# Attention of layer B with the keys on partitions in packed tiles, softmax sums from a ones matrix, and a layernorm by Ln and Exp

## The chip, the cores and the metric

The kernel runs on one core of one Trainium2 chip. The metric is the device time of one execution in microseconds (us). A kernel is run several times and its median is quoted. Engines are called as the profile calls them: PE is TensorE's matmul stream, PEld its weight loads, DVE is VectorE, ACT is ScalarE, POOL is GpSimd.

## The reference, cut to what matters

The network is four layers, A, B, A, B, each with a layernorm before it and a residual. Layer A is a Fourier filter and the change does not touch it, apart from the layernorm that it shares. Layer B is attention over 64 segments of 32 tokens. Each segment has 8 memory tokens in front of it, and they are the output of the segment before.

```python
# S = 2048 tokens, Dm = 640, H = 32 heads, Dh = 128, M = 8, seg_len = 32
for s in range(n_seg):                       # 64 segments
    h = concatenate([mem, x[:, s*32:(s+1)*32]], axis=1)      # 40 rows
    q, k, v = (einsum('btd,dhe->bhte', h, W) for W in (Wq, Wk, Wv))
    scores = where(mask, q @ k.T * Dh**-0.5, -1e9)
    o = einsum('bhte,hed->btd', softmax(scores) @ v, Wo)
    mem = o[:, :M]
    outs.append(o[:, M:])
```

Both kernels break the chain of segments in the same way. They guess the memories of all segments at once, run one pass over all segments, and compare the memories that come out with the guess. If the check fails, further, slower passes run on a branch.

## The kernel before: the parts that the argument touches

Before, layer B packs three segments into a window of up to 106 rows (3 x 32 tokens, 3 memory columns and 7 rows in front), and there are 22 windows. Heads are taken in pairs, because the values of two heads fill one 256-column matmul. The scores have the queries on partitions, so each softmax runs along the free axis, and the probabilities must be transposed before they can meet V.

```python
def vproj(w):                                # V of two heads: 22 windows x 5 chunks = 110 matmuls
    Vh = [vp.tile([128, 12, 256], BF16, name="V", tag="V") for _ in range(2)]
    for w0 in range(0, NW, 2):
        V, wv = Vh[w0 // 12], w0 % 12
        ps = pj.tile([128, 512], FP32, name="psv", tag="pj")          # pj: 3 banks
        for wi in range(2):
            for ch in range(5):
                nc.tensor.matmul(ps[:SZ, wi * 256:(wi + 1) * 256],
                                 lhsT=hT[:, ch, (w0 + wi) * ST:(w0 + wi) * ST + SZ],
                                 rhs=w["Wv"][:, ch, :], start=(ch == 0), stop=(ch == 4))
        nc.scalar.copy(out=V[:SZ, wv:wv + 2, :].rearrange("p a b -> p (a b)"), in_=ps[:SZ, :])
    return Vh
# ... cut: Q and K chains (psqk, 425 columns, both copied out by ScalarE) ...

for w0, nw in chunks:                        # 8 + 8 + 6 windows, per head
    # ... cut: tiles and views ...
    for i in range(nw):                      # scores, queries on partitions
        nc.tensor.matmul(bank(pss, i)[:SZ], lhsT=QT[:, t0:t0 + SZ], rhs=KT[:, t0:t0 + SZ], start=True, stop=True)
    nc.vector.tensor_tensor(out=v8(Sm)[:SZ], in0=view(pss)[:SZ], in1=mk, op=ALU.add)
    nc.vector.tensor_reduce(out=mx[:SZ, :nw], in_=Sm[:SZ, :nw, :], axis=AX.X, op=ALU.max)
    nc.vector.tensor_tensor(out=Sm[...], in0=Sm[...], in1=mx[...], op=ALU.subtract)
    nc.scalar.activation(out=E[:SZ, :nw, :], in_=Sm[:SZ, :nw, :], func=ACTF.Exp)
    nc.vector.tensor_reduce(out=sme[:SZ, :nw], in_=E[:SZ, :nw, :], axis=AX.X, op=ALU.add)
    nc.vector.reciprocal(out=sme[:SZ, :nw], in_=sme[:SZ, :nw])
    nc.vector.tensor_tensor(out=E[...], in0=E[...], in1=sme[...], op=ALU.mult)
    for i in range(nw):
        nc.tensor.transpose(out=pst[:SZ, i, :], in_=E[:SZ, i, :], identity=ident[:SZ, :SZ])
    nc.scalar.copy(out=PT[:SZ, :nw, :], in_=pst[:SZ, :nw, :])
    for i in range(nw):
        nc.tensor.matmul(bank(pso, i), lhsT=Vh[...][...], rhs=PT[:SZ, i, :], start=True, stop=True)
    nc.scalar.copy(out=v8(oTx), in_=view(pso)[:, :, :, XO:SZ])
    # ... cut: memory columns, store ...
```

Three other places matter. Before the attention of the last head, three banks are filled with output-projection matmuls of the first 28 heads, which are ready. At the start of layer B the normalised tokens are transposed, and each tile of transposes is copied out by one engine. The layernorm takes a square root on ScalarE and a reciprocal on VectorE.

```python
if oT0 is not None and h == H - 1:           # fill for the last head
    for j in range(3):
        pre[j] = pj.tile([128, 512], FP32, name="psx", tag="pj")
        xproj(pre[j], oT0, j, 0, 512, 0, HPRE)                        # HPRE = 28 heads
# in transpose_all: one engine for each chunk's bank
eng = nc.vector.tensor_copy if c % 2 == 0 else nc.scalar.copy
eng(out=dst, in_=ps[:, :, 0:6 * n].rearrange("p s (w j) -> p w j s", j=6))
# in _ln_apply
nc.scalar.activation(out=rs[:, :nt], in_=mv[:, :nt, 1], func=ACTF.Sqrt, bias=eps_t[:, 0:1])
nc.vector.reciprocal(out=rs[:, :nt], in_=rs[:, :nt])
```

Of the kernel before, what the change touches and what calls it, by code (L numbers as in the profile page):

```python
# [9 lines left out]
FP32 = mybir.dt.float32  # L10
BF16 = mybir.dt.bfloat16
# [73 lines left out]
def _ln_apply(nc, pool, mv, xin, xout, nt, eps_t, on_dve=False):  # L85
    rs = pool.tile([128, 4], FP32, name="lnrs", tag="lnrs")
    nb = pool.tile([128, 4], FP32, name="lnnb", tag="lnnb")
    nc.scalar.activation(out=rs[:, :nt], in_=mv[:, :nt, 1], func=ACTF.Sqrt, bias=eps_t[:, 0:1])
    nc.vector.reciprocal(out=rs[:, :nt], in_=rs[:, :nt])
# [191 lines left out]
TAIL_HEADS = 2  # L281


class _Lay:

    def __init__(self, dedup):
        self.dedup = dedup
        self.MR = 1 if dedup else MEM
        self.PRE = MEM - 1 if dedup else 0
        self.ST = 3 * self.MR + XW  # L290
        self.SZ = self.PRE + self.ST
        self.XO = self.PRE + 3 * self.MR
        self.NT = (NW - 1) * self.ST + self.SZ
        self.NM = self.PRE + NSEG * self.MR
        self.NMP = self.PRE + 3 * NW * self.MR
        self.NC = self.PRE + (NSEG - 1) * self.MR
        self.NR = (NW - 1) * self.ST + self.XO + SEG
        self.NB = 5 if dedup else 6
        self.BN = -(-self.NR // self.NB)
        assert self.BN * self.NB <= self.NT and self.BN <= 512 and 4 * self.SZ <= 512  # L300

    def mask(self, first):
        SZ, PRE, MR, XO = self.SZ, self.PRE, self.MR, self.XO
        seg = np.full(SZ, -1)
        pos = np.zeros(SZ, dtype=int)
        wgt = np.zeros(SZ)
        for a in range(3):
            seg[PRE + MR * a:PRE + MR * (a + 1)] = a
            pos[PRE + MR * a:PRE + MR * (a + 1)] = np.arange(MR) if MR > 1 else MEM - 1
            wgt[PRE + MR * a:PRE + MR * (a + 1)] = np.log(float(MEM // MR))  # L310
            seg[XO + SEG * a:XO + SEG * (a + 1)] = a
            pos[XO + SEG * a:XO + SEG * (a + 1)] = MEM + np.arange(SEG)
        if first and PRE:
            seg[0:PRE] = 0
            pos[0:PRE] = np.arange(PRE)
            wgt[PRE] = 0.0
        ok = (seg[:, None] == seg[None, :]) & (seg[None, :] >= 0) & ((pos[:, None] < MEM) | (pos[:, None] >= pos[None, :]))
        return np.where(ok, wgt[None, :], -1e9).astype(np.float32)

    def mask_tables(self):  # L320
        m0, m1 = self.mask(True), self.mask(False)
        return np.stack([m0] + [m1] * 7, 1), m1[:, None, :]


def _b_load_masks(tc, pool, lay, nm, gate=None):
    nc = tc.nc
    out = []
    for i, t in enumerate(lay.mask_tables()):
        m = pool.tile(list(t.shape), FP32, name=f"mask{nm}{i}")
        if gate is not None:  # L330
            _gate(nc, m[0:1, 0, 0:1], gate)
        nc.gpsimd.dma_start(out=m[:], in_=nc.inline_tensor(np.ascontiguousarray(t), name=f"mask_{nm}{i}_{pool.name}").ap())
        out.append(m)
    return out


def _b_prologue(tc, g, lay, hT, gq, xn_src, mem0):
    nc = tc.nc
    ident = g["ident"]
    ST, SZ, XO, PRE, MR = lay.ST, lay.SZ, lay.XO, lay.PRE, lay.MR  # L340
    with ExitStack() as ctx:
# [12 lines left out]
        nc.vector.memset(hw[:, :, :, PRE:XO], 0.0)  # L354
# [4 lines left out]
        nc.vector.tensor_copy(out=gq[:, :, 0:MR], in_=psm[:, 0, :, MEM - MR:MEM])  # L359
# [10 lines left out]
def _b_scatter(nc, lay, hT, gq):  # L370
    ST, XO, PRE, MR = lay.ST, lay.XO, lay.PRE, lay.MR
    n = NW - 1
    nc.vector.tensor_copy(out=hT[:, :, 0:n * ST].rearrange("p c (w t) -> p c w t", t=ST)[:, :, :, PRE:XO],
                          in_=gq[:, :, 0:3 * n * MR].rearrange("p c (w t) -> p c w t", t=3 * MR))
    nc.vector.tensor_copy(out=hT[:, :, n * ST + PRE:n * ST + PRE + MR], in_=gq[:, :, 3 * n * MR:NSEG * MR])


def _b_full_pass(tc, g, lay, env, flag_col):
    nc = tc.nc
    hT, gq, mnb, masks, oTm = env["hT"], env["gq"], env["mnb"], env["masks"], env["oTm"]  # L380
    Wo_sb, ident, ones_c, eps_t = g["Wo_sb"], g["ident"], g["ones_c"], g["eps"]
    oTx_d = g["oTx_d"]
    ST, SZ, XO, PRE, MR, NT, NM, NC = lay.ST, lay.SZ, lay.XO, lay.PRE, lay.MR, lay.NT, lay.NM, lay.NC
# [7 lines left out]
    with ExitStack() as ctx:  # L391
        wp = ctx.enter_context(tc.tile_pool(name="b1_w", bufs=2))
        vp = ctx.enter_context(tc.tile_pool(name="b1_v", bufs=4))
        qk = ctx.enter_context(tc.tile_pool(name="b1_qk", bufs=1))
        sm = ctx.enter_context(tc.tile_pool(name="b1_sm", bufs=2))
        oT0 = None
        if lay.dedup:
            oT0 = g["big"].tile([128, H, 512], BF16, name="oT0", tag="big")
        HPRE = H - 4
        pre = {}  # L400

        def xproj(ps, oTx, j, c0, c1, h0, h1):
            for h in range(h0, h1):
                nc.tensor.matmul(ps[:, 0:c1 - c0], lhsT=oTx[:, h, j * 128:(j + 1) * 128], rhs=Wo_sb[:, h, c0:c1], start=(h == 0), stop=(h == H - 1))  # L404
        BN = lay.BN
        wv_ = lambda t, o, w0_, n_: t[:, o + ST * w0_:o + ST * (w0_ + n_)].rearrange("p (w t) -> p w t", t=ST)

        def qk_evac(n, out, in_):
            if n == "Wq":
                nc.scalar.mul(out=out, in_=in_, mul=scale)  # L410
            else:
                nc.scalar.copy(out=out, in_=in_)

        def qk_chain(w, n, hh, ps, rhs_of):
            for ch in range(5):
                nc.tensor.matmul(ps, lhsT=w[n][:, ch, hh * 128:(hh + 1) * 128], rhs=rhs_of(ch), start=(ch == 0), stop=(ch == 4))  # L416

        def proj_full(w, hh, T2):
            for blk in range(lay.NB):
                for n in ("Wq", "Wk"):  # L420
                    ps = pj.tile([128, 512], FP32, name="psqk", tag="pj")
                    bn = min(BN, lay.NR - blk * BN)
                    qk_chain(w, n, hh, ps[:, :bn], lambda ch: hT[:, ch, blk * BN:blk * BN + bn])
                    qk_evac(n, T2[n][:, blk * BN:blk * BN + bn], ps[:, :bn])

        def proj_x(w, hh, T2):
            for w0_ in range(0, NW, 5):
                n_ = min(5, NW - w0_)
                for n in ("Wq", "Wk"):
                    if w0_ + n_ == NW:  # L430
                        ps = pj.tile([128, 512], FP32, name="psqk", tag="pj")
                        qk_chain(w, n, hh, ps[:, :(n_ - 1) * XW], lambda ch: wv_(hT[:, ch, :], XO, w0_, n_ - 1)[:, :, 0:XW])
                        c0_ = XO + ST * (NW - 1)
                        qk_chain(w, n, hh, ps[:, (n_ - 1) * XW:(n_ - 1) * XW + SEG], lambda ch: hT[:, ch, c0_:c0_ + SEG])
                        qk_evac(n, wv_(T2[n], XO, w0_, n_ - 1)[:, :, 0:XW], ps[:, :(n_ - 1) * XW].rearrange("p (w t) -> p w t", t=XW))
                        qk_evac(n, T2[n][:, c0_:c0_ + SEG], ps[:, (n_ - 1) * XW:(n_ - 1) * XW + SEG])
                        continue
# [401 lines left out]
```

## Time and profile before

| | before |
|---|---|
| median of 3 runs | 1954.84 us (1953.46 to 1956.66) |
| span of the profiled run, granted clock | 1956.5 us, 0.978 |
| period of one head pair in the attention loop (32 pairs in two layers) | 39.03 us |
| PE, ACT and DVE busy in one pair | 38.33, 29.80 and 27.36 us |

The first part of the profile page of the kernel before gives each engine's busy time, its share of the span, and its number of instructions.

```profile
PE 1840.5 (94%) x16192; PEld 1323.4 (68%) x16193; DVE 1143.5 (58%) x1810; ACT 1123.3 (57%) x2171; POOL 25.3 (1%) x50
```

PE is the fullest engine, but an average over the whole span mixes stages. The windows view of the kernel before shows one stage at a time. The columns are the stretch and its length; the busy us (and count) of PE, PEld, DVE, ACT and POOL; the granted clock; the DMA share; GB/s. The first line is one head pair in the middle of layer B's second pass. The second line runs from the V projection of the last pair to about the end of the second layer's attention and memory matmuls.

```profile
1293.75:1332.79 39.04, 38.33 (x344) 28.09 (x342) 27.36 (x36) 29.80 (x57) 0.00 (x0) 1.00 0.19 59
1741.70:1826.00 84.30, 73.01 (x646) 48.66 (x643) 42.10 (x66) 50.24 (x126) 0.00 (x0) 0.94 0.13 43
```

In the first line PE is busy 98% of the pair, while ACT and DVE have 9 and 12 us left. The waits view of the kernel before, over two pairs, says the same in another way. Its columns are the total of the waits in us, how many, and the longest.

```profile
DVE Sm L516 <- PE pss L509: 18.6, 2, 9.3
...
PEld L532 <- DVE E L528: 3.4, 8, 0.6
...
PE pst L532 <- DVE E L528: 0.3, 2, 0.2
```

DVE waits 9.3 us in each pair for PE to deliver scores. PE and its loader wait for E, but only 3.7 us in two pairs. This decides a question that the chain of waits leaves open. The fourth part of the page of the kernel before follows the last work back from its end, and its shares of the span are these:

```profile
PE 24%; DVE 20%; ACT 3%; DMA 1%; issue 1%; SPq 0%; DVEq 0%; ACTq 0%
PE psqk L416 7%; PE psx L404 7%; DVE Sm L516 4%; DVE sme L526 4%; DVE Sm L523 3%; DVE E L528 3%; DVE mx L517 3%; PE psv L458 2%; ACT E L525 1%; PE pst L532 1%; PE pso L536 1%; PE psu L215 1%; PE psg L244 1%; ACT PT L533 1%; DVE YT L72 1%
```

The chain runs through the softmax on DVE, because each head's softmax is a chain of dependent steps. Yet while it runs, PE is full of other heads' projections. A chain through an engine that then stands idle for 9 us a pair does not make that engine the limit.

The costliest groups of the page of the kernel before that the change removes or shrinks are below. The columns are line, engine, operation, tiles, shapes and count; busy us and the mean ns of one; idle time just before them and what ended it.

```profile
L458 PE MATMUL psv<-wWv,hTf 128*106 128x256 bf16 x3520 | 428.8, 273 | 2.2 <-ACT V L460 2.2
...
L526 DVE TENSOR_REDUCE sme<-E 106x8 f32<-106x848 bf16 (+1 forms) x192 | 182.4, 950 | 82.1 <-ACT E L525 60.3
...
L533 ACT COPY PT<-pst 106x848 bf16<-106x848 bf16 (+1 forms) x192 | 156.0, 812 | 83.1 <-PE pst L532 83.1
...
L532 PE MATMUL pst<-ident,E 106*106 106x106 bf16 x1408 | 107.5, 219 | 10.4 <-DVE E L528 4.4
```

The mean of 273 ns is the length of one matmul from start to end, and neighbours overlap. What a matmul costs a full PE is its spacing, start to start. When nothing waits, 256 columns take 109 ns in this trace. The Trainium skill, "TensorE: Matmul & The Clock Gate", section "Back-to-back issue gap", gives N / 2.4 + 2.5 ns for N columns as the gap of an isolated matmul (for a sustained stream it has other figures). In this document the sum of such spacings, worked out with columns / 2.4 + 2.4 ns, is called PE's floor, and the spacing above it is called gaps.

### The profile page before, as it was taken

What the parts mean: (1) busy time and instruction counts of PE and PEld (TensorE: products, weight loads), DVE (VectorE), ACT (ScalarE), POOL (GpSimd) and SP (SyncE); (2) the same over time, 40 slices, a digit from 0 to 9 for tenths busy, and PEclk for the clock granted to TensorE, in tenths of its full rate; (3) what the DMA queues carried; (4) which work ended last, traced back from release to release, by engine and by line L of the source; (5) the groups of instructions that cost most, each with busy time, mean ns of one, the idle gap of its engine ahead of it and who ended that gap; (6) DMA issues with size and microseconds to landing.
All of it is one profiled execution on the core that took longest, in us unless ns stands there. A gap on an engine that the chain in (4) does not pass through costs nothing. (4 is left out here: it accounts for less than half of the span.)

```text
span 1956.5 us, 38278 instructions
## 1 busy us (share of the span) xinstructions
PE 1840.5 (94%) x16192; PEld 1323.4 (68%) x16193; DVE 1143.5 (58%) x1810; ACT 1123.3 (57%) x2171; POOL 25.3 (1%) x50
## 2 busy tenths in 40 slices
PE   5988999999999999989969989999999999998898
PEld 3656866776677667567746568677667766774675
DVE  5555477765776577443355645777577757773211
ACT  4334577777777777620033437777777777775200
POOL 0100000000000000000000000000000000000000
PEclk8998999999999999999989989999999999999999
DMA  5752121212122211056172621221212121210630
GB/s 133 194 215 95 38 67 44 79 50 65 55 67 62 64 47 55 30 177 201 53 170 57 234 77 45 60 65 61 68 44 76 52 66 54 67 43 22 229 127 29
DMA packets 159149, 168.11 MB, mean 86 GB/s; under 512 B 9288, under 2 KB 146776, under 8 KB 157424
## 3 DMA queue, kind: packets, MB, share of 16 engines
q1 hardware_dynamic: 152832, 138.99, 22.3%
q0 software_dynamic: 6128, 26.51, 5.1%
q8 instruction: 130, 2.13, 0.4%
q14 instruction: 59, 0.48, 0.1%
HBM read 122.46 MB, written 52.95 MB: 90 GB/s over the span
## 5 line engine op out<-in xcount | busy, mean ns | idle before, releaser
L458 PE MATMUL psv<-wWv,hTf 128*106 128x256 bf16 x3520 | 428.8, 273 | 2.2 <-ACT V L460 2.2
L458 PEld LDWEIGHTS <-hTf 128*106 128x106 bf16 x3520 | 373.9, 128 | 2.5 <-issue 2.5
L416 PE MATMUL psqk<-hTf,wWk 128*128 128x425 bf16 (+5 forms) x1660 | 354.0, 337 | 3.4 <-ACT QT_25167 L410 1.7
L416 PE MATMUL psqk<-hTf,wWq 128*128 128x425 bf16 (+5 forms) x1660 | 354.5, 338 | 0.0
L460 ACT CAST V<-psv 106x512 bf16<-106x512 f32 x352 | 207.5, 603 | 67.7 <-PE psv L458 64.8
L416 PEld LDWEIGHTS <-wWq 128*128 128x128 bf16 x1660 | 155.0, 98 | 115.4 <-issue 0.8
L416 PEld LDWEIGHTS <-wWk 128*128 128x128 bf16 x1660 | 153.1, 98 | 117.8 <-issue 4.7
L526 DVE TENSOR_REDUCE sme<-E 106x8 f32<-106x848 bf16 (+1 forms) x192 | 182.4, 950 | 82.1 <-ACT E L525 60.3
L404 PE MATMUL psx<-Wo_sb,oTxl 128*128 128x320 bf16 x1536 | 209.0, 299 | 0.0
L533 ACT COPY PT<-pst 106x848 bf16<-106x848 bf16 (+1 forms) x192 | 156.0, 812 | 83.1 <-PE pst L532 83.1
L404 PEld LDWEIGHTS <-oTxl 128*128 128x128 bf16 x1536 | 150.3, 98 | 58.3
L528 DVE TENSOR_TENSOR E<-E,sme 106x848 bf16<-106x848 bf16 (+1 forms) x192 | 184.0, 959 | 3.4
L517 DVE TENSOR_REDUCE mx<-Sm 106x8 f32<-106x848 f32 (+1 forms) x192 | 182.1, 948 | 1.3
L523 DVE TENSOR_TENSOR Sm<-Sm,mx 106x848 f32<-106x848 f32 x180 | 173.0, 961 | 1.1
L525 ACT ACTIVATE E<-Sm 106x848 bf16<-106x848 f32 x180 | 157.4, 874 | 16.8 <-DVE Sm L523 16.8
L539 ACT CAST oTx<-pso 128x768 bf16<-128x768 f32 (+1 forms) x192 | 145.3, 757 | 13.2 <-PE pso L536 7.2
L604 DVE TENSOR_TENSOR xo<-psx,xr 128x320 bf16<-128x320 f32 (+2 forms) x64 | 31.3, 491 | 180.9 <-PE psx L404 174.6
L516 DVE TENSOR_TENSOR Sm<-pss,maskf_23870 106x848 f32<-106x848 f32 x32 | 33.2, 1038 | 154.5 <-PE pss L509 154.5
L516 DVE TENSOR_TENSOR Sm<-pss,maskf_890 106x848 f32<-106x848 f32 x32 | 33.2, 1038 | 154.5 <-PE pss L509 154.5
L532 PEld LDWEIGHTS <-E 106*106 106x106 bf16 x1408 | 86.9, 131 | 52.6 <-DVE E L528 50.4
L536 PEld LDWEIGHTS <-V 106*128 106x128 bf16 x1408 | 87.5, 98 | 49.2 <-issue 43.4
L532 PE MATMUL pst<-ident,E 106*106 106x106 bf16 x1408 | 107.5, 219 | 10.4 <-DVE E L528 4.4
(603 smaller groups left out, 2087.0 us busy)
## 6 DMA issues: line engine op xcount, KB each, us to landing
oTx_d<-oTx SPq DMA_DIRECT2D x128, 192.0 KB, 1.9
oTxl<-oTx_d SPq DMA_DIRECT2D x24, 1024.0 KB, 8.2
Wv_sb<-in_B_Wv_dram POOLq DMA_DIRECT2D x10, 1024.0 KB, 9.5
wWq<-in_B_Wq_dram SPq DMA_DIRECT2D x32, 320.0 KB, 3.3
wWk<-in_B_Wk_dram SPq DMA_DIRECT2D x32, 320.0 KB, 3.7
wWv<-in_B_Wv_dram SPq DMA_DIRECT2D x32, 320.0 KB, 4.0
oTx_d<-oTx SPq DMA_DIRECT2D x64, 144.0 KB, 1.8
Wo_sb<-in_B_Wo_dram POOLq DMA_DIRECT2D x4, 1280.0 KB, 9.3
```

The source lines that it names most:

```text
L404: nc.tensor.matmul(ps[:, 0:c1 - c0], lhsT=oTx[:, h, j * 128:(j + 1) * 128], rhs=Wo_sb[:, h, c0:c1], start=(h == 0), stop=(h == H - 1))
L416: nc.tensor.matmul(ps, lhsT=w[n][:, ch, hh * 128:(hh + 1) * 128], rhs=rhs_of(ch), start=(ch == 0), stop=(ch == 4))
L458: nc.tensor.matmul(ps[:SZ, wi * 256:(wi + 1) * 256], lhsT=hT[:, ch, (w0 + wi) * ST:(w0 + wi) * ST + SZ], rhs=w["Wv"][:, ch, :], start=(ch ...
L460: nc.scalar.copy(out=V[:SZ, wv:wv + 2, :].rearrange("p a b -> p (a b)"), in_=ps[:SZ, :])
L517: nc.vector.tensor_reduce(out=mx[:SZ, :nw], in_=Sm[:SZ, :nw, :], axis=AX.X, op=ALU.max)
L523: nc.vector.tensor_tensor(out=Sm[:SZ, :nw, :], in0=Sm[:SZ, :nw, :], in1=mx[:SZ, :nw].unsqueeze(2).to_broadcast([SZ, nw, SZ]), op=ALU.subtract)
L525: nc.scalar.activation(out=E[:SZ, :nw, :], in_=Sm[:SZ, :nw, :], func=ACTF.Exp)
L526: nc.vector.tensor_reduce(out=sme[:SZ, :nw], in_=E[:SZ, :nw, :], axis=AX.X, op=ALU.add)
L528: nc.vector.tensor_tensor(out=E[:SZ, :nw, :], in0=E[:SZ, :nw, :], in1=sme[:SZ, :nw].unsqueeze(2).to_broadcast([SZ, nw, SZ]), op=ALU.mult)
L532: nc.tensor.transpose(out=pst[:SZ, i, :], in_=E[:SZ, i, :], identity=ident[:SZ, :SZ])
L533: nc.scalar.copy(out=PT[:SZ, :nw, :], in_=pst[:SZ, :nw, :])
L539: nc.scalar.copy(out=v8(oTx), in_=view(pso)[:, :, :, XO:SZ])
```

## The change

The intent is to give PE fewer columns and DVE far less work. Eight things in the diff matter here.

1. The keys of all 64 segments are packed into 17 tiles of 128, so V needs 85 matmuls a pair instead of 110.
2. The scores have the keys on partitions, so their exponentials are already laid out for the product with V. The transposes and their copies go.
3. No maximum is subtracted. The mask is multiplied in after the exponential.
4. A matmul with a matrix of ones gives the softmax sum on every partition; ScalarE turns it into its inverse by exp(-ln(sum)), and DVE multiplies that into the output.
5. Since nothing bounds the exponentials now, the range is checked after the fact: the score Exps also give accumulated sums, and POOL adds them, and a row of the inverse sums, into two accumulators.
6. The projections have 2 PSUM banks instead of 3. The fill of the last head goes.
7. The layernorm takes exp(-0.5 ln(var)) and one refining step, so that all functions are in one ScalarE table.
8. The outputs of the last two heads stay in SBUF for the output projection; the others still go to DRAM and come back, as all did before.

The core of the diff, with cuts:

```diff
+ones128, accR [1,512], accE [128,9]          # ... cut: constants and packing tables ...
+            elif h % 2 == 0:
+                v_pair(w, h // 2)             # 17 tiles; nc.scalar.copy evacuates 512 columns
+            q_all(w, h); k_all(w, h)          # Q leaves by ScalarE, K by VectorE
+            P = scores(h)
+            if todo is not None:
+                values(*todo)                 # sums and values of the head before
+            todo = (h, P)
# scores, in 9 parts of at most 283 columns
-nc.vector.tensor_tensor(add mask); tensor_reduce(max); tensor_tensor(subtract)
-nc.scalar.activation(Exp); tensor_reduce(add); reciprocal; tensor_tensor(mult)
-nc.tensor.transpose(...); nc.scalar.copy(PT <- pst)
+nc.tensor.matmul(ps[:, ...], lhsT=KT[:, t * 128:(t + 1) * 128], rhs=QT[:, lo:hi], start=True, stop=True)
+nc.scalar.activation(out=E[:, 0:n], in_=ps[:, 0:n], func=ACTF.Exp, accum_out=eE[:, i:i + 1])
+nc.vector.tensor_tensor(out=P[:, o0:o0 + n], in0=E[:, 0:n], in1=bs.mask[:, o0:o0 + n], op=ALU.mult)
# after 9 parts:
+nc.gpsimd.tensor_tensor(out=accE[:], in0=accE[:], in1=eE[:], op=ALU.add)
# values, in 5 groups of at most 502 columns; banks: psl 2, pso 2, pss 2
+matmuls psl <- ones128, P ; pso <- V, P
+nc.scalar.activation(out=L[:, 0:n], in_=psl[:, 0:n], func=ACTF.Ln, bias=g["floor"][:, 0:1])
+nc.scalar.activation(out=R[:, 0:n], in_=L[:, 0:n], func=ACTF.Exp, scale=-1.0)
+nc.gpsimd.tensor_tensor(out=accR[:, 0:n], in0=accR[:, 0:n], in1=R[0:1, 0:n], op=ALU.add)
+nc.vector.tensor_tensor(out=oT[...], in0=v(pso)[...], in1=v(R)[...], op=ALU.mult)
+nc.vector.tensor_tensor(out=oTm[...], in0=v(pso)[:, :, SEG], in1=v(R)[:, :, SEG], op=ALU.mult)
# transposes at the start of layer B: the packing cuts each bank into 8 copies, by both engines
-eng(out=dst, in_=ps[:, :, 0:6 * n]...)
+for g_ in range(4):
+    (nc.vector.tensor_copy if g_ % 2 == 0 else nc.scalar.copy)(out=dst, in_=src)
+# ... cut: four smaller copies of the same bank, two by each engine ...
# layernorm
-nc.scalar.activation(Sqrt); nc.vector.reciprocal
+nc.scalar.activation(Ln); nc.scalar.activation(Exp, scale=-0.5); four small VectorE operations
```

## The prediction

> **What bounds the kernel now.** TensorE. The page has PE busy 94% of 1956.5 us, DVE 58%, ACT 57%. Layer B's attention loop (16 head pairs, run twice) takes about 2 x 625 us. The chain of waits repeats every 39.03 us, one pair. A window of one pair has PE busy 38.3 us, ACT 29.8, DVE 27.4, at full clock. By the start-to-start spacing of matmuls in two such windows a pair is: V 110 x 109 ns = 12.0 us; Q and K 100 x 180 ns = 18.0; scores, transposes, values 132 x about 50 ns = 6.6; the other 2.4 us are waits, mostly for DVE's E and ACT's PT.
>
> **What the change does to a pair.**
> - PE. V: 17 full tiles instead of 22: 85 x 109 ns = 9.3 us (-2.7). Q/K: 2129 columns instead of 2121: 18.0. Transposes go; scores, ones-matrix sums and values each stream 2253 columns in 18 matmuls a head, at the rate of the V matmuls (256 columns in 109 ns) 0.98 us each, 5.9 a pair (-0.7). Sum 33.2 us before waits, against 36.6.
> - DVE. Max, subtract, sum and normalise go (each about 1 us per 848 columns). K evacuation, a mask multiply and the multiply by the inverse sum come: estimate 21 us, from the 491 ns of a 320-column PSUM add.
> - ACT. PT and oT copies and K evacuation go; Ln and Exp over 2119 columns a head and nine Exps a head with accumulated sums come. From 0.83 ns a column and 0.17 to 0.26 us fixed (512-column cast 587 ns, 24-column cast 190 to 205): V 5.1, Q 5.8, score Exps 7 plus 1 to 3.5 for reading accumulators, Ln and Exp of sums 11.7: 31 to 33 us, about what PE has.
> - POOL gets about 6 us of small adds a head, hidden.
>
> PE's floor falls by 3.4 us a pair, but ACT rises to the same level, and its work is bunched: 19 activations a head (10 to 11 us), while PE has 3 us of attention matmuls. With two projection banks (three before) PE can run two further Q or V chains before it waits for ACT; K chains leave ACT idle. I expect 36 to 37 us a pair, -80 us in all.
>
> **Outside the loop.** Before, the last head's softmax wait is filled with output-projection matmuls (73 in 15.8 us in the chain). That goes, and the last head's Exp, Ln, Exp chain is exposed: +5 to 8 us a layer. Layernorm loses table loads of 1283 ns and a reciprocal, gains four small DVE ops and an ACT op: +3 us exposed. The Trainium skill ("ScalarE: Activation LUTs", Table sets) says Ln and Exp share a set; four loads are in this trace, I expect one. That page states one element per cycle whatever the function; the 848-column Exp (about 0.9 us) agrees.
>
> **Prediction.** 1880 us, 8 in 10 between 1800 and 1965. Faster by over 2%: 0.68; within 2%: 0.17; slower: 0.15. The fallback branch should not run.
>
> **What would show it.** Right: V spacing still 109 ns, 85 a pair; no transposes; period 36 to 37 us; in the loop ACT at least 85% busy, PE about 90%, PE's waits ended by ACT (projection and score banks), DVE under 65%. Wrong: matmuls of 132 columns spaced well over 57 ns; ACT outside 30 to 34 us a pair; waits ended by DVE or POOL.
>
> **What would make it wrong.** If the order keeps ACT evenly fed, the period nears 34 us (about 1800). If ACT's attention work and PE's projections alternate instead of overlapping, it passes 40 us and the change loses. A long accumulator read would do the same, or an R buffer held by slow POOL adds.

## The result, and the profile after

| | before | after |
|---|---|---|
| median (4 runs each, same chip) | 1955.75 us | 1906.31 us (1905.05 to 1907.81) |
| ratio | | 0.9744, 95% interval 0.9730 to 0.9757 |
| span of the profiled run, clock | 1956.5 us, 0.978 | 1903.3 us, 0.981 |
| period of a head pair | 39.03 us | 37.45 us |

All outputs were correct, and the fallback branch did not run.

The first part of the page of the kernel after:

```profile
PE 1743.0 (92%) x14586; PEld 1183.3 (62%) x14587; DVE 906.0 (48%) x2786; ACT 1006.3 (53%) x2844; POOL 384.4 (20%) x436
```

PE lost 97.5 us of busy time, and the span only 53. ACT, which the prediction expected to rise to PE's level, has less busy time than before. The windows view of the kernel after, one pair and the tail of the second layer up to the last memory matmul (1758.1) and a little beyond:

```profile
1289.83:1327.28 37.45, 35.44 (x296) 23.62 (x294) 19.16 (x62) 26.29 (x81) 11.23 (x12) 1.00 0.21 70
1701.97:1760.20 58.23, 51.70 (x545) 36.00 (x542) 28.85 (x99) 38.63 (x122) 19.74 (x21) 1.00 0.22 72
```

The groups of the page of the kernel after that answer to those of before, and the new ones:

```profile
L760 POOL TENSOR_TENSOR accR<-accR,R 1x495 f32<-1x495 f32 (+2 forms) x320 | 343.6, 1074 | 700.1 <-ACT R L759 689.9
L723 PE MATMUL psv<-wWv,hTf 128*128 128x256 bf16 x2720 | 334.5, 272 | 5.1 <-DVE hTf L901 2.4
...
L758 ACT ACTIVATE L<-psl,floor 128x495 f32<-128x495 f32 (+2 forms) x320 | 195.5, 627 | 7.3 <-PE psl L754 7.3
L759 ACT ACTIVATE R<-L 128x495 f32<-128x495 f32 (+2 forms) x320 | 180.3, 577 | 5.5 <-POOL accR L760 2.4
...
L754 PE MATMUL psl<-P,ones_72 128*128 128x132 bf16 (+8 forms) x1152 | 133.7, 218 | 42.9 <-ACT L L758 32.6
...
L739 ACT ACTIVATION_READ_ACCUMULATOR E<-pss 128x1 f32 x576 | 123.0, 214 | 0.0
```

V has 2720 matmuls instead of 3520, of the same length. The sum matmuls (`psl`) have 42.9 us of idle PE before them, and most of it (32.6 us) ends with an Ln: in this program a sum bank is free only when its Ln has read it. The waits view of PE in the kernel after, over two pairs:

```profile
PE psl L754 <- ACT L L758: 2.1, 4, 0.6
PE pso L754 <- DVE oTmf L767: 1.1, 2, 0.5
PE psl L754 <- ACT QT_25579 L664: 0.5, 2, 0.2
```

### One pair, by kind of matmul

These spacings are worked out from the start times of the matmuls in the two traces, over two pairs, in us a pair; the floor has 26 ns, as measured, for the few matmuls of 5 columns.

| | before: spacing | floor | after: spacing | floor |
|---|---|---|---|---|
| Q and K | 18.84 | 17.91 | 18.13 | 17.90 |
| V | 13.29 | 12.00 | 10.17 | 9.27 |
| scores | 2.46 | 2.05 | 2.06 | 2.00 |
| transposes | 2.32 | 2.05 | none | none |
| sums | none | none | 3.98 | 2.00 |
| values | 2.13 | 2.05 | 3.04 | 2.00 |
| whole pair | 39.04 | 36.06 | 37.45 | 33.18 |

(The spacings of the kernel after add up to 37.38, since one V matmul of 170 falls outside the stretch or is missing from the trace.) The floor fell by 2.9 us, and the gaps rose from 3.0 to 4.3, so the period fell by 1.6. The largest gaps after are 1.40 us between sum matmuls, 0.69 before the values that follow V matmuls, and 0.41 and 0.39 after values.

### The whole span

Landmarks in the two profiled runs cut the span into pieces without remainder.

| piece | before | after | difference |
|---|---|---|---|
| start to the first guess matmul of layer B's first pass | 179.8 | 187.4 | +7.6 |
| from there to the third pair's V, both layers | 169.8 | 171.2 | +1.4 |
| 13 periods, both layers | 1014.9 | 973.9 | -41.0 |
| last pair's V to the last output-projection matmul, both layers | 412.5 | 386.2 | -26.3 |
| from there to the first guess matmul of the second layer B | 170.9 | 176.4 | +5.5 |
| end | 8.6 | 8.2 | -0.4 |
| sum | | | -53.2 |

Two of these were not foreseen. In the +7.6 and +5.5, the stretch from the first token transpose to the first guess matmul grew from 9.5 and 9.4 us to 13.4 and 14.0. And the tail, for which the prediction had a loss, gained 13.1 us a layer, of which only 1.6 is the shorter period.

### The profile page after: what moved, and what is told of

The parts are those of the page before. It is cut to its first block, busy times and chain, and to the rows that moved or that the text cites. A ratio compares the mean times of both kernels' runs of the same rounds, so it can differ in the third digit from the quotient of the medians.

```text
span 1903.3 us, 38101 instructions
## 1 busy us (share of the span) xinstructions
PE 1743.0 (92%) x14586; PEld 1183.3 (62%) x14587; DVE 906.0 (48%) x2786; ACT 1006.3 (53%) x2844; POOL 384.4 (20%) x436
## 5 line engine op out<-in xcount | busy, mean ns | idle before, releaser
L760 POOL TENSOR_TENSOR accR<-accR,R 1x495 f32<-1x495 f32 (+2 forms) x320 | 343.6, 1074 | 700.1 <-ACT R L759 689.9
L723 PE MATMUL psv<-wWv,hTf 128*128 128x256 bf16 x2720 | 334.5, 272 | 5.1 <-DVE hTf L901 2.4
L739 ACT ACTIVATE E<-pss 128x269 bf16<-128x269 f32 (+5 forms) x576 | 216.9, 390 | 206.1 <-PE pss L736 178.6
L657 PE MATMUL psq<-hTf,wWq 128*128 128x128 bf16 (+3 forms) x1560 | 304.8, 335 | 2.6 <-ACT QT_2048 L675 0.4
L657 PE MATMUL psk<-hTf,wWk 128*128 128x495 bf16 (+3 forms) x1600 | 303.8, 342 | 0.0
L723 PEld LDWEIGHTS <-hTf 128*128 128x128 bf16 x2720 | 256.9, 97 | 40.3 <-issue 6.3
L765 DVE TENSOR_TENSOR oT<-pso,R 128x480 bf16<-128x480 f32 (+1 forms) x320 | 185.8, 581 | 80.0 <-ACT R L759 60.5
L740 DVE TENSOR_TENSOR P<-E,maskf 128x269 bf16<-128x269 bf16 (+5 forms) x576 | 178.9, 326 | 51.8 <-ACT E L739 37.7
L758 ACT ACTIVATE L<-psl,floor 128x495 f32<-128x495 f32 (+2 forms) x320 | 195.5, 627 | 7.3 <-PE psl L754 7.3
L759 ACT ACTIVATE R<-L 128x495 f32<-128x495 f32 (+2 forms) x320 | 180.3, 577 | 5.5 <-POOL accR L760 2.4
L754 PE MATMUL psl<-P,ones_72 128*128 128x132 bf16 (+8 forms) x1152 | 133.7, 218 | 42.9 <-ACT L L758 32.6
```

What stands on the lines that cost most here:

```text
L657: nc.tensor.matmul(ps, lhsT=w[:, ch, hh * 128:(hh + 1) * 128], rhs=src[:, ch, lo:hi], start=(ch == 0), stop=(ch == 4))
L723: nc.tensor.matmul(ps[:, i * 256:(i + 1) * 256], lhsT=hT[:, ch, (t + i) * 128:(t + i + 1) * 128], rhs=w["Wv"][:, ch, :], start=(ch == 0), ...
L739: nc.scalar.activation(out=E[:, 0:n], in_=ps[:, 0:n], func=ACTF.Exp, accum_out=eE[:, i:i + 1])
L740: nc.vector.tensor_tensor(out=P[:, o0:o0 + n], in0=E[:, 0:n], in1=bs.mask[:, o0:o0 + n], op=ALU.mult)
L754: nc.tensor.matmul(dst[:, lo - q0:hi - q0], lhsT=lhs(t), rhs=P[:, off:off + hi - lo], start=(i == 0), stop=(i == len(mine) - 1), skip_grou ...
L758: nc.scalar.activation(out=L[:, 0:n], in_=psl[:, 0:n], func=ACTF.Ln, bias=g["floor"][:, 0:1])
```

## Experiments

The theories for the loop:

- **A**: ScalarE gates PE. Its work comes in bursts, and a V copy that stands in front of an Ln delays the Ln that frees a sum bank.
- **B**: the accumulated exponentials gate PE, through the 214 ns reads of the accumulator on ScalarE.
- **C**: the POOL adds gate PE, because they slow DVE or hold a buffer.
- **D**: two projection banks are too few. This is what the prediction said.

A caution for all of them. The instructions of each engine are put in order when the kernel is built, and one edit can change the order elsewhere. So the order of the 293 PE matmuls of one pair was compared with that of the kernel after. The column "same order" says how many of them lie in blocks that a program for comparing texts matches, by kind of matmul alone. It is a rough measure: the longest sequence that two orders share is 268 for a1_vdve, 232 to 256 for the others that changed, and 293 for a3_nopool and d2_trans.

| label | edit to the kernel after, unless said | median us | ratio to before | pair period us | same order |
|---|---|---|---|---|---|
| (after) | | 1906.31 | 0.9744 | 37.45 | 293 |
| a1_vdve | V copied by VectorE | 1871.72 | 0.9573 | 36.35 | 237 |
| a2_noacc | no accumulated exponentials | 1899.36 | 0.9714 | 37.53 | 177 |
| a3_nopool | no POOL add of the inverse sums | 1884.43 | 0.9639 | 37.01 | 293 |
| a4_pj3 | 3 projection banks, 1 sum bank | 1906.24 | 0.9756 | 37.67 | 149 |
| b1_v17 | kernel before, V of 17 windows | 5894.77 | 3.0102 | 36.33 | not compared |
| b2_ln | kernel before, layernorm of after | 1955.52 | 0.9987 | 39.04 | not compared |
| a6_rbuf4 | 4 buffers for R | 1919.76 | 0.9809 | 38.13 | 172 |
| c1_accsum | a1, and sums of R by ScalarE | 1869.07 | 0.9550 | 36.36 | 151 |
| d1_order | values between Q and K | 1890.72 | 0.9659 | 37.12 | 163 |
| d2_trans | transposes copied by one engine a tile | 1899.03 | 0.9698 | 37.45 | 293 |
| d3_all | c1, d1 and d2 | 1865.03 | 0.9530 | 36.72 | 229 |
| d4_notreorder | c1 and d2 | 1862.21 | 0.9519 | 36.36 | 151 |

The runs of the kernel before that went with each call had medians of 1955.08, 1957.56, 1957.24 and 1956.59 us, so a difference of two medians from different calls is uncertain by some 2 us. All outputs were correct.

### a1_vdve: does the V copy on ScalarE delay the Ln?

The timeline of the kernel after shows the two waits for an Ln that each pair has. Its columns are start in us, length, engine, line, operation, tiles, and in brackets the idle time before it and what ended it.

```profile
1293.42 0.61 ACT L759 ACTIVATE R<-L 128x495 f32<-128x495 f32 x1
...
1293.93 0.37 ACT L758 ACTIVATE L<-psl,floor 128x132 f32<-128x132 f32 x1
...
1294.18 0.59 ACT L725 CAST V<-psv 128x512 bf16<-128x512 f32 x1
...
1294.35 0.40 PE L754 MATMUL psl<-P,ones_72 128*128 128x132 bf16 x4 [0.48 <-ACT L L758]
...
1307.28 0.64 PE L754 MATMUL psl<-P,ones_72 128*128 128x132 bf16 x8
1307.78 0.67 ACT L758 ACTIVATE L<-psl,floor 128x495 f32<-128x495 f32 x1 [0.24 <-PE psl L754]
1308.50 0.24 PE L754 MATMUL psl<-P,ones_72 128*128 128x5 bf16 x2 [0.58 <-ACT L L758]
```

At 1294.35 PE had stood for 0.48 us at a sum matmul until an Ln ended. In front of that Ln ScalarE had the Exp of R, and before it score Exps; the copy of V comes behind the Ln. At 1308.50 PE had filled both sum banks in a row (8 matmuls) and stood for 0.58 us while an Ln, for which ScalarE had been idle, took its own 0.67 us. So at neither wait does V stand in front, as theory A has it. Over the whole trace the sum matmuls have 98 gaps above 0.1 us, and in none is there a copy of V in the unbroken run of ScalarE work that leads up to the Ln.

```diff
-nc.scalar.copy(out=V[:, t:t + n, :].rearrange("p a b -> p (a b)"), in_=ps[:, 0:n * 256])
+nc.vector.tensor_copy(out=V[:, t:t + n, :].rearrange("p a b -> p (a b)"), in_=ps[:, 0:n * 256])
```

> The changed kernel with V evacuated by VectorE instead of ScalarE; one edit, nothing removed. In the changed kernel's trace a pair takes 37.45 us, its matmuls need 33.1 us of streaming (columns over 2.4 GHz plus 2.4 ns each), 4.1 us are gaps. Theory A (ScalarE order: V's evacuation stands behind attention's Exp and Ln in ScalarE's queue, so the two projection banks fill and PE is left with matmuls that wait for ScalarE): gaps fall by 1 us a pair or more, period 36.5 us or less, whole about 1875 us. Rival B (accumulator reads), C (POOL adds hold R) and D (too few banks, whoever empties them): the period stays within 0.4 us[...].

Measured: 1871.72 us, ratio 0.9573 (0.9557 to 0.9589), period 36.35 us. The windows view of a1_vdve over two pairs:

```profile
1270.56:1343.31 72.75, 70.16 (x589) 47.22 (x587) 49.06 (x142) 44.48 (x141) 22.48 (x24) 1.00 0.19 65
```

The waits view of PE in a1_vdve over the same stretch:

```profile
PE pso L754 <- DVE oTmf L767: 1.1, 2, 0.5
PE psl L754 <- ACT QT L664: 0.6, 2, 0.3
PE psl L754 <- ACT L L758: 0.6, 2, 0.3
```

The wait of the sum matmuls for an Ln fell from 2.1 to 0.6 us in two pairs, and the gap between sum matmuls from 1.40 to 0.45 us a pair. All gaps (the period less the floor of 33.18) fell from 4.3 to 3.2 us, close to the 3.0 of before the change. The gain of 1.10 us a pair times 32 pairs is 35 us, and the time fell by 34.6. The number is the one that theory A forecast, but its mechanism is not what the traces show. The order moved too: at the first of the two waits, 20 V matmuls and 4 of the values now lie between two groups of sums that stood side by side, and that gap (0.65 us) is gone; at the second, 4 of the values lie between, and 0.75 us became 0.45. So what the traces show is a better order of PE, which gives each Ln time to read its bank. No run moves V's copy with the order kept, so whether the copy itself cost anything stays open.

### a2_noacc: do the accumulated exponentials cost?

```diff
-nc.scalar.activation(out=E[:, 0:n], in_=ps[:, 0:n], func=ACTF.Exp, accum_out=eE[:, i:i + 1])
+nc.scalar.activation(out=E[:, 0:n], in_=ps[:, 0:n], func=ACTF.Exp)
-nc.gpsimd.tensor_tensor(out=accE[:], in0=accE[:], in1=eE[:], op=ALU.add)
```

> The changed kernel without the accumulator output of the score Exps and without the add of it (results stay right, the range check of the exponentials is weaker). It removes 18 accumulator reads of 214 ns a pair, in start-to-start time about 0.09 us each. Theory A: score Exps free their banks sooner, but the gaps that count are at the sums' banks: 0 to 0.5 us a pair. Rival B (accumulator reads are what PE waits for): 1.5 us a pair or more, about 1855 us.

Measured: 1899.36 us, ratio 0.9714 (0.9698 to 0.9731), period 37.53 us. Eighteen reads of 214 ns a pair went, and the period did not fall. The 7 us did not come from the steady pairs. Theory B falls as a cause of the period in the order that this run had; as the order changed much (177 of 293), it says little about a fixed order.

### a3_nopool: are the POOL adds hidden?

```diff
-nc.gpsimd.tensor_tensor(out=accR[:, 0:n], in0=accR[:, 0:n], in1=R[0:1, 0:n], op=ALU.add)
```

> The changed kernel without POOL's adds of the inverse sums (320 of 1.07 us on the page; results stay right, that part of the range check never fires). Rival C (a POOL add keeps one of two R buffers, so ScalarE's second Exp and with it everything behind waits): period down by 0.5 us or more. Theory A: period unchanged within 0.2 us; only the end of each layer gains, where the chain of waits shows two POOL adds of 1.24 us and one of 0.46: 2 to 4 us a layer, whole about 1900 us.

Measured: 1884.43 us, ratio 0.9639 (0.9623 to 0.9655), period 37.01 us. PE's order in the pair is exactly that of the kernel after, so this is the cleanest of the runs. The gap before the values that follow V fell from 0.69 to 0.06 us a pair. The timeline of the kernel after shows how an add on POOL made it:

```profile
1291.33 1.22 POOL L760 TENSOR_TENSOR accR<-accR,R 1x495 f32<-1x495 f32 x1 [4.45 <-ACT R L759]
...
1291.79 1.12 DVE L740 TENSOR_TENSOR P<-E,maskf 128x253 bf16<-128x253 bf16 x2
...
1292.83 0.16 DVE L767 TENSOR_TENSOR oTmf<-pso,R 128x15 bf16<-128x15 f32 x1
...
1293.05 0.24 PE L754 MATMUL pso<-P,V 128*128 128x5 bf16 x2 [0.53 <-DVE oTmf L767]
```

From top to bottom: POOL reads its row of R, two mask multiplies on DVE, 1.12 us together, lie in the same time and one of them is stretched, the small multiply behind them starts late, and PE waits 0.53 us for the bank that it frees. In the by-form view of the kernel after, the multiplies of 253 columns are slower than the longer ones of 269 columns, which rarely meet an add:

```profile
L740 DVE TENSOR_TENSOR P<-E,maskf 128x269 bf16<-128x269 bf16 x192 | 58.4, 304 | 17.0 <-ACT E L739 9.7
...
L740 DVE TENSOR_TENSOR P<-E,maskf 128x253 bf16<-128x253 bf16 x128 | 55.8, 436 | 19.0 <-ACT E L739 18.7
```

In the by-form view of a3_nopool the same group is:

```profile
L740 DVE TENSOR_TENSOR P<-E,maskf 128x253 bf16<-128x253 bf16 x128 | 36.8, 288 | 18.6 <-ACT E L739 18.3
```

One by one, 34 of the 576 mask multiplies of the kernel after took about 0.91 us instead of 0.29; all 34 overlap such an add, and without the adds there is none above 0.311 us. The Trainium skill, "SBUF — State Buffer", section "Who interferes with whom", says: "A DVE instruction with two SBUF inputs contends with a GpSimd instruction that reads SBUF". The mask multiply has two such inputs, and the trace agrees. The multiply that makes `oT` has one input in PSUM, and it is not stretched: 0.657 us in the median for the 136 full-sized ones that overlap an add, 0.655 for the other 120.

So theory C is right in part: the adds cost 0.44 us a pair, which is 14 us in 32 pairs, and 2.7 us more in each tail (190.4 instead of 193.1 us from the last pair's V to the last output-projection matmul). It was not the larger part of the gaps, since PE still waited 2.5 us in two pairs for an Ln; the gap between sum matmuls even grew from 1.40 to 1.60 us a pair, which took back a part of the 0.63 us won before the values.

### a4_pj3: are two projection banks too few?

```diff
-pj = tile_pool(name="b_pj", bufs=2, space=PSUM)
+pj = tile_pool(name="b_pj", bufs=3, space=PSUM)
-psl = pa.tile([128, 512], FP32, name="psl", tag="psl")           # 2 banks
+psl = pa.tile([128, 512], FP32, name="psl", tag="psl", bufs=1)
# ... cut: the same in the output projection ...
```

> The changed kernel with three projection banks and one bank for the sums (psl) instead of two and two. Theory D and my own prediction (two projection banks are too few): period 36.5 us or less. Theory A, by which the sums' banks are what PE is stuck at: with one bank every group of sums waits for the Ln before it, so gaps at psl grow from 1.4 us a pair to 3 or more unless the order puts projections there; period 37 to 39 us.

Measured: 1906.24 us, ratio 0.9756 (0.9738 to 0.9775), period 37.67 us. The run takes the third projection bank from the sums, so it weighs one against the other. It gives no support to theory D. In the kernel after, PE's waits were at the sum and value banks and not at the projection banks. Nor did the wait at the sums grow, as theory A's text had it: in the order of this run PE waited for an Ln 0.4 us in two pairs with one sum bank (2.1 us with two in the kernel after), and its longest total was 1.4 us for a value bank. So the order decided more than the number of sum banks.

### b1_v17: is V's saving whole where nothing else changes?

The kernel before with V computed for 17 of its 22 windows, and the other windows using V of the first ones.

```diff
-for w0 in range(0, NW, 2):
+for w0 in range(0, 17, 2):
-                         lhsT=Vh[(w0 + i) // 12][:SZ, (w0 + i) % 12, ...]
+                         lhsT=Vh[((w0 + i) % 17) // 12][:SZ, ((w0 + i) % 17) % 12, ...]
```

> The kernel before with V computed for 17 of its 22 windows, the other five reading the first windows' V (wrong result on purpose), which is the changed kernel's count of V matmuls (85 a pair, not 110) without its attention. Theory V (the streaming that the change saves is V's, 2.7 of 2.9 us a pair; the new attention saves almost none and its gaps are larger): period 36.0 to 36.8 us instead of 39.03, whole 1865 to 1885 us, that is, faster than the changed kernel. Rival (the new softmax is where the time came from): V's matmuls only fill waits, period 38 us or more, whole above 1925 us.

Measured: 5894.77 us, three times the time of before. The wrong values made the memory check fail, so the slow passes of the fallback ran, and the whole time says nothing. (The output still passed, since the fallback passes compute again.) The first pass is still readable. Its period is 36.33 us, 2.70 less than before, and V's floor fell by 25 x 109 ns = 2.7 us. One pair of that first pass in the windows view of b1_v17:

```profile
367.00:403.30 36.30, 35.69 (x321) 25.36 (x319) 27.33 (x38) 28.04 (x56) 0.00 (x0) 1.00 0.18 58
```

DVE has as much to do as before (27.33 us against 27.36), and the period fell by all that PE lost. ScalarE lost copies of V as well (28.04 us busy against 29.80), but it had been idle for 9 us of each pair. So PE was the limit of the loop before, and not the DVE softmax through which the chain of waits runs.

### b2_ln: the layernorm alone

The kernel before with the Ln and Exp layernorm and the table loaded at the start.

```diff
-nc.scalar.activation(out=rs[:, :nt], in_=mv[:, :nt, 1], func=ACTF.Sqrt, bias=eps_t[:, 0:1])
-nc.vector.reciprocal(out=rs[:, :nt], in_=rs[:, :nt])
+nc.scalar.activation(out=r0, in_=mv[:, :nt, 1], func=ACTF.Ln, bias=eps_t[:, 0:1])
+nc.scalar.activation(out=r0, in_=r0, func=ACTF.Exp, scale=-0.5)
+# ... cut: four small VectorE operations, one refining step ...
+nc.scalar.preload_act_table_set(...)          # at the start: the set that has both
```

> The kernel before with the layernorm of the change alone (Ln, Exp, one Newton step; the table set with both). The trace shows the changed kernel 7.6 us later at the start of the first guess and 5.5 us slower from the end of the first layer B to the second guess, of which 4 us each lie between the first transpose and the guess. Layernorm theory: the rest, 3 to 5 us in all, is layernorm's: whole 1955 to 1962 us. Rival: dropping three table loads makes it neutral or faster, 1950 to 1955.

Measured: 1955.52 us, ratio 0.9987 (0.9970 to 1.0003), period 39.04 us. The layernorm is neutral. In the profiled run the first token transpose came 4.0 us later than before (174.3 against 170.3), as in the kernel after (174.0), and as much or a little more came back later, in the first pairs, the tail and the end. So the rise of 3.7 us ahead of the first transpose belongs to this part or to its scatter: among the kernels that share this layernorm the first transpose comes between 172.2 and 174.8 us.

### a6_rbuf4: do the POOL adds hold the buffer of R?

```diff
-R = sm.tile([128, 512], FP32, name="R", tag="R")                 # 2 buffers
+R = sm.tile([128, 512], FP32, name="R", tag="R", bufs=4)
```

> The changed kernel with four R buffers instead of two, POOL's adds kept. The run without the adds won 0.44 us a pair. Rival C (an add holds an R buffer): four buffers win the same, period about 37.0. Theory P ([...]one mask multiply a pair takes 0.92 us instead of 0.29 while an add runs, and PE's bank for the values waits behind it): period within 0.2 us of 37.45 unless the order itself changes, and the longest mask multiply still about 0.9 us.

Measured: 1919.76 us, ratio 0.9809 (0.9793 to 0.9826), period 38.13 us: slower than the kernel after. The 34 stretched multiplies remain, and PE waits longer for Ln, 2.7 us in two pairs. More buffers gave the build another order (172 of 293), and a worse one. That the adds hold R is not supported, but a run whose order changed so much can't exclude it.

### c1_accsum: both remedies

V on VectorE, and the sum of the inverse sums taken by ScalarE with the Exp that makes them, so that POOL has one small add a head.

```diff
-nc.scalar.activation(out=R[:, 0:n], in_=L[:, 0:n], func=ACTF.Exp, scale=-1.0)
-nc.gpsimd.tensor_tensor(out=accR[:, 0:n], in0=accR[:, 0:n], in1=R[0:1, 0:n], op=ALU.add)
+nc.scalar.activation(out=R[:, 0:n], in_=L[:, 0:n], func=ACTF.Exp, scale=-1.0, accum_out=eR[:, g_:g_ + 1])
+# once a head: accR [128, 5] += eR, on POOL
# ... cut: the check that reads accR, and the edit of a1_vdve ...
```

> A candidate that keeps the whole check: the changed kernel with V evacuated by VectorE, and the sum of inverse sums taken by ScalarE's accumulator output of the Exp that makes R, with one POOL add of 128x5 a head instead of five of up to 1x502. If the two gains add (1.09 and 0.44 us a pair), the period is 35.7 to 36.1 us and the whole 1848 to 1862 us; ten more accumulator reads a pair cost ScalarE about 1 us of 24.5, which is not on the chain. If they overlap: no better than 1870.

Measured: 1869.07 us, ratio 0.9550 (0.9534 to 0.9566), period 36.36 us. No multiply is stretched any more, yet the period is that of a1_vdve (36.35), whose ratio interval overlaps with this one. The two gains in the loop do not add. With the adds gone and V on VectorE, PE's order is new again (151 of 293), and what is left of the gaps has other causes.

### d1_order: sums and values among the projections

```diff
 q_all(w, h)
+values(h - 1)                # sums and values of the head before
 k_all(w, h)
-P = scores(h)
-values(h - 1)
-todo = (h, P)
+todo = (h, scores(h))
```

> The changed kernel with one move: the sums and values of the previous head are issued between the Q and the K projections of a head, not after its scores. In the changed kernel's trace ScalarE stands idle for 3.0 and 1.6 us of each head's K projections (which VectorE empties), and right after them has nine Exps, and Ln and Exp of the sums, to do at once. Theory A (bunched ScalarE work is what PE waits for): Ln and Exp fill the K stretch, the gaps at the sums' banks fall from 2 us a pair to under 1, period 36.0 to 36.6, whole 1860 to 1880. Rival (a sum's Ln takes about 0.7 us, PE's four matmuls 0.25, and the two banks give this wait wherever the sums stand): period 37.2 or more.

Measured: 1890.72 us, ratio 0.9659 (0.9645 to 0.9674), period 37.12 us. The period lies between what its theory A and the rival said. The waits at the sums fell, and a new one came, as the waits view of PE in d1_order shows over two pairs:

```profile
PE psk L657 <- DVE KT L714: 2.7, 4, 0.9
...
PE psl L754 <- ACT L L758: 0.5, 2, 0.3
```

K chains now run among the values, and DVE is busy with those when a K bank should be copied. A wait was traded for another.

### d2_trans: the transposes at the start of the layer

In the kernel after, each tile of transposed tokens is copied out in eight pieces by both engines. (The code cuts and the recorded texts call this tile a bank; it has twice the bytes of the attention's 512-column fp32 tiles, which are one bank each, and all but two small copies read from its whole length.) The timeline of the kernel after:

```profile
1117.25 0.66 DVE L887 COPY hTf<-pstr 128x480 bf16<-128x480 bf16 x1 [1.55 <-PE pstr L882]
1117.94 0.56 ACT L887 COPY hTf<-pstr 128x480 bf16<-128x480 bf16 x1 [2.16 <-DVE hTf L887]
...
1122.28 1.99 PE L882 MATMUL pstr<-ident,xna 128*128 128x128 bf16 x17 [2.49 <-DVE hTf L894]
```

ACT starts only when DVE has ended: the copies of one tile take turns. The Trainium skill, "PSUM — Partial Sum Buffer", section "Terms", under PSUM bank, says that two engines on the same bank and quadrant at once are an error, "reads against reads included". The order in the trace agrees with this. The timeline of the kernel before, where one engine has a tile for itself, shows the two engines side by side:

```profile
1141.93 2.26 DVE L666 COPY hTf<-pstr 128x2016 bf16<-128x2016 bf16 x1 [1.55 <-PE pstr L663]
1143.69 1.84 ACT L666 COPY hTf<-pstr 128x2016 bf16<-128x2016 bf16 x1 [3.23 <-PE pstr L663]
```

The experiment gives each tile to one engine again and joins three of the eight copies into one:

```diff
-self.hT = fp.tile([128, 5, st.NK], BF16, name="hTf")
+self.hT = fp.tile([128, 5, st.NK + 4], BF16, name="hTf")
+eng = nc.vector.tensor_copy if c % 2 == 0 else nc.scalar.copy
-(nc.vector.tensor_copy if g_ % 2 == 0 else nc.scalar.copy)(out=dst, in_=src)
+eng(out=dst, in_=src)
# ... cut: the last four segments in one copy, the four tail columns in another, both by eng ...
```

> The changed kernel with the transposed rows of one PSUM bank copied out by one engine (VectorE and ScalarE take turns by bank, as in the kernel before), not by both in turn, and 6 copies a bank instead of 8. From the first transpose to the guess the kernel before takes 9.4 us, the changed one 13.4 and 14.0. If sharing a bank between two engines that take turns is the loss: 9.5 to 11 us, 6 to 9 us in the whole, ratio to before about 0.970; the loop unchanged at 37.45. Rival (the number of copies, 40 against 10): little gain, 12 us or more.

Measured: 1899.03 us, ratio 0.9698 (0.9685 to 0.9711); the loop is unchanged at 37.45 us and in the same order. The timeline of d2_trans:

```profile
1115.41 2.35 DVE L888 COPY hTf<-pstr 128x480 bf16<-128x480 bf16 x4 [1.55 <-PE pstr L882]
1116.79 1.95 ACT L888 COPY hTf<-pstr 128x480 bf16<-128x480 bf16 x4 [2.84 <-PE pstr L882]
```

Both engines wait for PE only, and their copies overlap. From the first transpose to the first guess matmul takes 9.8 and 9.7 us instead of 13.4 and 14.0, so 7.8 of the 8.5 us lost in two layers came back, and the time fell by 7.3 (9 by the two ratios). It took away two short copies a tile as well, so a small part may be theirs; with 30 copies instead of 40 (10 before) the rival, the number of copies, is no more than that.

### d3_all and d4_notreorder: putting them together

d3_all has the edits of c1_accsum, d1_order and d2_trans; d4_notreorder has those of c1_accsum and d2_trans, without the new order.

> A candidate of all that helped: V emptied by VectorE, accumulated inverse sums instead of POOL's long adds, the sums and values issued before K, and the transposes by bank. c1 had 36.36 us a pair and 1869 us. Without interplay: period 35.3 to 36.0, 7 us less outside, whole 1830 to 1852. If the gains overlap as POOL's did with V's: 1855 to 1865.

> The candidate without the move of the sums: V emptied by VectorE, accumulated inverse sums, transposes by bank. The move raised the period from 36.36 (c1) to 36.72 us when it stood beside the other two edits, and lowered it from 37.45 to 37.12 alone. If that is all there is to it: period 36.36, 8 us less outside the loop than c1, whole 1859 to 1863 us, the fastest of all. If the transposes' gain does not add: 1866 to 1870.

Measured: d3_all 1865.03 us, ratio 0.9530 (0.9515 to 0.9544), period 36.72 us; PE waits 2.1 us in two pairs for DVE's copy of K. d4_notreorder 1862.21 us (1861.51 to 1863.44), ratio 0.9519 (0.9506 to 0.9532), period 36.36 us. Both periods are outside what the text of d3_all hoped for (35.3 to 36.0); d4_notreorder came out as forecast. The new order, a gain by itself, is a loss when V's copies are on DVE as well. The windows view of d4_notreorder over two pairs:

```profile
1262.00:1335.00 73.00, 71.01 (x590) 47.81 (x589) 48.03 (x142) 46.59 (x163) 1.84 (x8) 1.00 0.19 64
```

PE is busy 97% of it. d4_notreorder is the fastest version: 4.8% under the kernel before by its ratio, where the change as given is 2.6% under it.

## Why the prediction was right or wrong

The time was inside the range (1906 against 1880, 1800 to 1965), and the sign was right. But the sum was right partly because errors cancelled: half of the gain (26.3 of 53.2 us) came from the tails, where the prediction had a loss. That part is luck. Even on its own terms it was loose: -80 in the loop, twice +5 to +8, and +3 make about -64, which is 1891 and not 1880.

- **PE is the limit before: right.** b1_v17 shows it. V's floor fell by 2.7 us and the period by 2.70, with DVE's work unchanged.
- **PE's floor falls by 3.4 us: a little too large.** V came out exactly (12.0 to 9.3). The attention matmuls had been costed at 50 ns each before, and their floor was 46.6, so the pair went from 36.06 to 33.18, by 2.9.
- **"31 to 33 us, about what PE has": this ScalarE term was mis-sized.** The durations of a pair's ScalarE instructions do add up to 34.0 us after (33.3 before), but its busy time is 26.3 us (29.8 before), because neighbours overlap: 62 of 79 instructions a pair start before the one in front has ended, by 0.12 us in the median. A part of the trace of the kernel after:

```profile
1291.05 0.41 ACT L739 ACTIVATE E<-pss 128x253 bf16<-128x253 f32 x1
...
1291.31 0.24 ACT L739 ACTIVATION_READ_ACCUMULATOR E<-pss 128x1 f32 x1
...
1291.40 0.43 ACT L739 ACTIVATE E<-pss 128x269 bf16<-128x269 f32 x1
```

  The read starts 0.15 us before the Exp ends, and the next Exp starts 0.15 us before the read ends. The Trainium skill, "ScalarE: Activation LUTs", section "What ACT_TABLE_LOAD costs", says "Back-to-back ACTIVATEs overlap by ≈ 93 ns"; the trace has 0.12 us, and the prediction used neither. ScalarE was 70% busy in the loop, not the predicted 85% or more; by the prediction's own signs ("ACT outside 30 to 34 us a pair") this term was wrong.
- **"PE's waits ended by ACT": right, for another reason.** It was not the total of ScalarE's work that counted, and the banks were those of the sums, not of projections and scores. PE came to a sum bank before the Ln that frees it had ended, once behind score Exps and the Exp of R, once with nothing in front. In a1_vdve's order other matmuls lie between the groups of sums, and the gaps went down to 3.2 us. A further 1.1 us in two pairs was a wait for DVE, which the prediction had among its signs of being wrong.
- **"Two projection banks instead of three, PE waits for ACT": not confirmed.** The waits of the kernel after are at the sum banks and at one value bank, and a4_pj3 was not faster.
- **Period 36 to 37 us, -80 us: too good.** The period is 37.45, so -1.58 us a pair: the floor gave 2.9 and the gaps took back 1.3. That would be -51 us in 32 pairs. The 26 periods that can be read directly gave -41.0, and the stretch with the first two pairs of each layer gave no gain (+1.4).
- **"POOL gets about 6 us of small adds a head, hidden": wrong.** They stretch DVE's mask multiplies from 0.29 to 0.91 us when the two meet, and one of these lies in front of an instruction that frees a bank that PE waits for. a3_nopool measured 22 us in all.
- **"The last head's chain is exposed: +5 to 8 us a layer": wrong in sign.** The tail gained 13.1 us a layer. In the timeline of the kernel before, the fill for the last head stands in front of that head's transposes on PE:

```profile
1790.40 15.92 PE L404 MATMUL psx<-Wo_sb,oT_25166 128*128 128x512 bf16 x73
...
1793.66 1.04 DVE L528 TENSOR_TENSOR E<-E,sme 106x848 bf16<-106x848 bf16 x1
...
1806.16 0.56 PE L532 MATMUL pst<-ident,E 106*106 106x106 bf16 x8
...
1806.81 0.87 ACT L533 COPY PT<-pst 106x848 bf16<-106x848 bf16 x1 [14.49 <-PE pst L532]
```

  E was ready at 1794.70, and its transposes came 11.5 us later, because PE was in one block of 73 fill matmuls; ScalarE waited 14.49 us in all. So the fill held the softmax up after it was ready, and little was left to cover its later steps. In these PE stood once for 6.10 us (up to 1814.81), by the profile until the last heads' outputs had come back from DRAM; the kernel after keeps the last two heads in SBUF, and PE has no wait for a DMA in its tail. From the last pair's V to the last memory matmul the stretch fell from 87.3 to 56.1 us, and the output projection that follows rose from 119 to 137 us, because the fill's work comes there now. PE's granted clock in the two tail windows shown above was 0.94 before and 1.00 after. No run isolates these parts, so the cause of the tail's gain is argued and not shown.
- **Layernorm +3 us: too large in the whole.** b2_ln is the same as before within its interval, though the first transpose came 4.0 us later there, and 3.7 us later in the kernel after. Four table loads of 1283 ns became one, as predicted, and as the skill's section "Table sets: the hidden batching unit" on the same page says of ln and exp.
- **Missing from the prediction: the transposes, +4.2 us a layer**, from copies of one tile by two engines that take turns. d2_trans confirmed it.

The failed terms nearly cancel. The loop gave -43 (-41.0, +1.4, and -3.2 as the last pairs' share of the tails) in place of -80, so 37 too little. The transposes cost 8.5 that were not foreseen. The rest of the tails gave -23 in place of +10 to +16, so 33 to 39 better. Together that is 6 to 12 us short of the terms, whose middle is -64, and the spans show -53.2.

What stays open: PE still has 3 us of gaps a pair in the best version. How much of that lies in the order in which the build puts the instructions and how much in the number of banks, these runs do not tell apart. Five of the single edits to the kernel after (a1_vdve, a2_noacc, a4_pj3, a6_rbuf4 and d1_order) changed PE's order as well, so only a3_nopool and d2_trans are clean measures of what they removed.

## What to carry to other kernels

When a full PE loses matmuls, the gain is what is left after the new waits, so list for each new PSUM bank which engine frees it, what stands in front of that instruction in that engine's queue, and what PE has to do in the meantime. An engine's load is its busy time and not the sum of its durations, and "hidden" work on POOL was not hidden here where DVE read two SBUF inputs beside it (0.29 us became 0.91). After each single edit, compare the order of the instructions before you believe that the difference in time is the edit's.

## What the Trainium skill lacked or had wrong

- "ScalarE: Activation LUTs": it does not give the cost of an accumulator output. Here each is a separate instruction of 214 ns in the mean (576 of them), and it overlaps each neighbour by 0.11 us in the median.
- "ScalarE: Activation LUTs", section "What ACT_TABLE_LOAD costs": back-to-back overlap is given as about 93 ns. Here the median over mixed instructions is 0.12 us, and 62 of 79 in a pair overlap. The 1283 ns of a table load agree exactly.
- "TensorE: Matmul & The Clock Gate", section "Back-to-back issue gap": it gives about 81 ns sustained for 128 columns with a weight load for each matmul. Here, with a weight load for each, 112 to 141 columns had spacings of about 50 to 65 ns where nothing waited, and 128 columns 55.5; the formula that the page keeps for an isolated gap fits.
- "SBUF — State Buffer", section "Who interferes with whom": the rule fits, but it has no size for this pair of instructions. Here a mask multiply of 0.29 us took about 0.91 us beside a POOL add of 495 columns on one partition (1.07 us in the mean).
- No page that was read says that a fill of matmuls put in front of a waiting step can delay that step; here 73 matmuls of 15.9 us kept transposes waiting for 11.5 us after their input was ready.
